# Row-half scores, a 0/1 mask product and a written instruction order in a sparse-attention plus mixer kernel

## The chip, the cores and the metric

The kernel runs on one core of one Trainium2 chip. The metric is the device time of one execution in microseconds (us). The kernel before takes 299.21 us, the median of three runs (299.06 to 299.65). A profile's span runs from the first to the last instruction and is some 2 us shorter than the time of the same execution.

## The reference, cut to what matters

```python
batch, n_heads, seq, head_dim = (4, 8, 768, 64)     # blocks of 32: 24 x 24 blocks
scores = q @ k.T / sqrt(D)
mask = |blk_i - blk_j| <= 1, first and last block row and column, 3 sampled blocks per row
attn = softmax(where(mask, scores, -1e9)) @ v
x = attn, heads side by side                        # (4, 768, 512)
u = x + (x.T @ U @ V).T                             # rank 32
out = u + relu(u @ w_ch1) @ w_ch2                   # 512 -> 2048 -> 512
```

Heads are handled in pairs: 4 pairs to a batch, 16 in all, numbered from 0.

## The kernel before: the parts that matter

The mask costs no instruction of its own in the steady state. Each head's transposed q and k fill 64 of the 128 rows that the array sums over. The other 64 rows hold a one-hot of the query block and a bias of -240 for masked block pairs, so one matmul gives score plus bias, and the exponential of a masked score is zero.

```python
def scores(i, h, g):                    # head h of pair i, 128 keys of row block g
    qT, kT = augs[i]                    # 64 data rows and 64 mask rows
    psc = pscp.tile([P, 2, 512], FP32, tag="psc", name="psc")   # 2 banks, double-buffered
    for c in range(2):
        nc.tensor.matmul(psc[:, c, 0:HS],
            kT[:, h, g * P : (g + 1) * P], qT[:, h, c * HS : (c + 1) * HS],
            start=True, stop=True)
    nc.scalar.activation(out=est[:, g]..., in_=psc[:, :, 0:HS], func=AF.Exp, scale=0.125)

def av(self, h, g): ...                 # value product: 6 matmuls of 65 columns a row block
def w1(jj, c): ...                      # hidden layer: 4 matmuls of 384 columns, then relu
def w2(sc, part): ...                   # output layer: 4 matmuls of 512 columns
# [cut]: PSUM pools: scores 2 x 2 banks, value product 1, everything else 3.
# [cut]: w1 and w2 steps are dealt evenly between the score slots of the next batch.
```

TensorE keeps the written order. On the other engines a scheduler chooses it, and the PSUM buffers come from pools.

The softmax here doesn't subtract the row's maximum and nothing guards it: scores larger than these inputs give would overflow.

## Time and profile before

| | before |
|---|---|
| time, median | 299.21 us |
| span | 296.7 us |
| TensorE, ScalarE, VectorE busy | 98%, 61%, 48% |
| exponentials, 768 columns | 192, one each 0.702 us where they follow each other |
| granted TensorE clock | 1.000 |

From the profile's page of the kernel before, the lines of busy time by engine and of the chain of waits (share of the span, by engine):

```profile
span 296.7 us, 6622 instructions
...
PE 291.4 (98%) x2775; PEld 182.3 (61%) x2775; DVE 142.0 (48%) x299; ACT 179.8 (61%) x261; POOL 50.2 (17%) x70
...
PE 87%; ACT 12%; issue 0%; DVE 0%
```

A busy TensorE is not yet a bound TensorE, so the chain is read next. It is followed backwards from the last instruction to whatever released each step. In order of time, for the kernel before (start, duration, engine, tile, line, count):

```profile
7.13 8.43 ACT est L392 x12
...
37.00 4.21 ACT est L392 x6
...
57.57 0.36 PE pv L426 x12
57.93 0.65 PE pm L509 x4
58.58 0.33 PE psc L386 x2
...
83.00 0.86 PE pm L531 x4
```

Until 42 us ScalarE is the chain: six exponentials take 4.21 us. From 48 us on only TensorE is on it, and these lines give its rates: 0.65/4 = 0.162 us for 384 columns, 0.86/4 = 0.215 us for 512, 0.36/12 = 0.030 us for a value-product matmul. The mean durations below are longer (325 ns for a score matmul) because matmuls overlap. Costs of TensorE must be taken from starts, not from durations.

Groups of the page: line, operation, shapes and count, then busy time and mean ns of one, then the idle time before them and its releaser.

```profile
L392 ACT ACTIVATE est<-psc 128x768 f16<-128x768 f32 x192 | 149.6, 812 | 51.6 <-PE psc L386 50.7
...
L386 PE MATMUL psc<-qres,kres 128*128 128x384 f16 x384 | 93.5, 325 | 1.0 <-ACT est L392 0.7
```

### The profile page before, as it was taken

What the parts mean: (1) busy time and instruction counts of PE and PEld (TensorE: products, weight loads), DVE (VectorE), ACT (ScalarE), POOL (GpSimd) and SP (SyncE); (2) the same over time, 40 slices, a digit from 0 to 9 for tenths busy, and PEclk for the clock granted to TensorE, in tenths of its full rate; (3) what the DMA queues carried; (4) which work ended last, traced back from release to release, by engine and by line L of the source; (5) the groups of instructions that cost most, each with busy time, mean ns of one, the idle gap of its engine ahead of it and who ended that gap; (6) DMA issues with size and microseconds to landing.
All of it is one profiled execution on the core that took longest, in us unless ns stands there. A gap on an engine that the chain in (4) does not pass through costs nothing.

```text
span 296.7 us, 6622 instructions
## 1 busy us (share of the span) xinstructions
PE 291.4 (98%) x2775; PEld 182.3 (61%) x2775; DVE 142.0 (48%) x299; ACT 179.8 (61%) x261; POOL 50.2 (17%) x70
## 2 busy tenths in 40 slices
PE   8999999999999999999999999999999999999995
PEld 3677776666666555666665556666665655565444
DVE  7766776346452525454452624346462535443112
ACT  5999997587766655767775555777875530332000
POOL 4773184014031212030201203030000000000000
PEclk9999999999999999999999999999999999999999
DMA  6899949096959494744719385662510121000111
GB/s 192 288 315 235 295 154 144 8 254 94 170 187 231 136 225 139 163 139 72 224 29 240 121 178 198 141 188 43 92 29 35 39 62 73 36 0 2 71 71 71
DMA packets 58661, 39.94 MB, mean 135 GB/s; under 512 B 40152, under 2 KB 55144, under 8 KB 58632
## 3 DMA queue, kind: packets, MB, share of 16 engines
q1 hardware_dynamic: 55764, 35.19, 43.9%
q0 software_dynamic: 2688, 4.19, 8.3%
q8 instruction: 21, 0.34, 0.5%
q10 hardware_dynamic: 180, 0.15, 0.1%
q14 instruction: 8, 0.07, 0.1%
HBM read 27.72 MB, written 6.29 MB: 115 GB/s over the span
## 4 chain that ended last, share of the span: by engine, by line
PE 87%; ACT 12%; issue 0%; DVE 0%
PE pm L509 28%; PE pm L531 27%; PE psc L386 16%; ACT est L392 12%; PE pv L426 9%; PE pm L448 1%; PE psc L218 1%; PE pm L481 1%; PE pm L550 1%; PE pm L527 0%; PE pm L497 0%; PE pm L364 0%; PE pm L201 0%; PE psc L201 0%; DVE of L555 0%
## 5 line engine op out<-in xcount | busy, mean ns | idle before, releaser
L392 ACT ACTIVATE est<-psc 128x768 f16<-128x768 f32 x192 | 149.6, 812 | 51.6 <-PE psc L386 50.7
L509 PE MATMUL pm<-uT,w1t 128*128 128x384 f16 x512 | 94.6, 326 | 0.0
L386 PE MATMUL psc<-qres,kres 128*128 128x384 f16 x384 | 93.5, 325 | 1.0 <-ACT est L392 0.7
L531 PE MATMUL pm<-w2t,tT 128*128 128x512 f16 x368 | 90.7, 379 | 0.0
L509 PEld LDWEIGHTS <-w1t 128*128 128x128 f16 x512 | 47.1, 98 | 27.0 <-issue 0.2
L426 PEld LDWEIGHTS <-est 128*128 128x128 f16 x1152 | 51.9, 97 | 16.5
L519 DVE TENSOR_SCALAR tT<-pm 128x384 f16<-128x384 f32 x64 | 35.6, 556 | 51.3 <-PE pm L509 48.6
L426 PE MATMUL pv<-vt,est 128*128 128x65 f16 x1152 | 55.7, 193 | 0.0
L517 ACT ACTIVATE tT<-pm 128x384 f16<-128x384 f32 x64 | 31.4, 490 | 38.2 <-PE pm L509 25.5
L386 PEld LDWEIGHTS <-kres 128*128 128x128 f16 x384 | 36.0, 97 | 27.0 <-issue 1.9
L531 PEld LDWEIGHTS <-tT 128*128 128x128 f16 x368 | 33.3, 98 | 30.1
L144 POOL CAST qst<-qld 128x768 f16<-128x768 f32 x10 | 8.3, 827 | 120.5 <-DMA qld<-in_q_dram 120.5
L539 DVE TENSOR_TENSOR of<-xf,pm 128x512 f32<-128x512 f32 x23 | 15.7, 684 | 25.9 <-PE pm L531 25.9
L435 DVE RECIPROCAL rcp<-pv 128x6 f32<-128x6 f32 x32 | 6.1, 192 | 38.1 <-PE pv L426 38.1
L440 DVE TENSOR_TENSOR xh<-pv,rcp 128x384 f16<-128x384 f32 x32 | 17.8, 557 | 1.0
L486 DVE TENSOR_TENSOR u<-xh,pm 128x384 f16<-128x384 f16 x24 | 13.2, 551 | 9.8 <-PE pm L481 9.3
L440 DVE TENSOR_TENSOR xf<-pv,rcp 128x384 f32<-128x384 f32 x32 | 17.5, 547 | 0.0
L154 POOL CAST vt<-vld 128x768 f16<-128x768 f32 x16 | 13.3, 828 | 14.7 <-DMA vld<-in_v_dram 14.2
L487 DVE TENSOR_TENSOR xf<-xf,pm 128x384 f32<-128x384 f32 x24 | 13.1, 547 | 0.0
L452 DVE CAST a<-pm 128x128 f16<-128x128 f32 x16 | 4.7, 291 | 15.9 <-PE pm L448 15.8
L144 POOL CAST kst<-kld 128x768 f16<-128x768 f32 x10 | 8.3, 827 | 5.1 <-DMA kld<-in_k_dram 5.1
L448 PE MATMUL pm<-xh,Ut 128*128 128x128 f16 x96 | 8.0, 219 | 0.0
(75 smaller groups left out, 111.2 us busy)
## 6 DMA issues: line engine op xcount, KB each, us to landing
vld<-in_v_dram SPq DMA_DIRECT2D x16, 384.0 KB, 5.3
out_dram<-of SPq DMA_DIRECT2D x23, 256.0 KB, 2.0
qld<-in_q_dram SPq DMA_DIRECT2D x15, 384.0 KB, 4.6
kld<-in_k_dram SPq DMA_DIRECT2D x15, 384.0 KB, 5.0
w1t<-in_moe_w_ch_dram POOLq DMA_DIRECT2D x4, 512.0 KB, 10.6
w2t<-in_moe_w_ch_dram POOLq DMA_DIRECT2D x4, 512.0 KB, 6.3
qld<-in_q_dram SPq DMA_DIRECT2D x2, 192.0 KB, 3.3
kld<-in_k_dram SPq DMA_DIRECT2D x2, 192.0 KB, 3.3
```

What stands on the lines that cost most here:

```text
L144: last = nc.gpsimd.tensor_copy(out=dst, in_=ld)
L154: nc.gpsimd.tensor_copy(out=vts[b % 2][:, 2 * hp : 2 * hp + 2, :, 0:D], in_=ld)
L386: nc.tensor.matmul(psc[:, c, 0:HS], kT[:, h, g * P : (g + 1) * P], qT[:, h, c * HS : (c + 1) * HS], start=True, stop=True,)
L392: nc.scalar.activation(out=est[:, g].rearrange("k (c n) -> k c n", c=2), in_=psc[:, :, 0:HS], func=AF.Exp, scale=0.125,)
L426: nc.tensor.matmul(pav[:, sc, :], est[:, g, sc * P : (sc + 1) * P], vts[self.b % 2][:, head, g, 0 : D + 1], start=(g == 0 and sc == 0), st ...
L440: self.last = nc.vector.tensor_tensor(out=dst, in0=pav[:, :, 0:D], in1=rcp[:, :, None].broadcast_to([P, T, D]), op=ALU.mult,)
L486: nc.vector.tensor_add(out=self.u16[:, ts, :], in0=self.xh[:, ts, :], in1=pu)
L509: nc.tensor.matmul(pt, w1t[:, cc, jj * P : (jj + 1) * P], bt.uT[cc][:, c * HS : (c + 1) * HS], start=(cc == 0), stop=(cc == NCC - 1),)
L517: nc.scalar.activation(out=dst, in_=pt, func=AF.Relu)
L519: nc.vector.tensor_scalar_max(out=dst, in0=pt, scalar1=0.0)
L531: nc.tensor.matmul(hold[sc], bt.tT[jj][:, sc * P : (sc + 1) * P], w2t[:, jj, :], start=(b > 0 and jj == 0), stop=(jj == NJJ - 1),)
L539: nc.vector.tensor_add(out=of, in0=bt.xf[:, sc, :], in1=hold[sc])
```

## The change

The intent is to take work off the bounding TensorE. From pair 4 on, a head's scores use only their 64 data rows, and the two heads of a pair stand in opposite halves of the array, to be multiplied at the same time. The mask can then no longer ride in the other rows. It is made once, by matmuls from zero-padded mask rows, as a 0/1 tile, and VectorE multiplies each exponential by it. One ScalarE instruction covers 1,536 columns. With the mask columns gone, the transposes of q and k by DMA are half as large. A "quad" below is two row blocks of both heads: eight matmuls, six of the eight PSUM banks, two exponentials, two mask products.

From pair 1's scores on, the order of all instructions on TensorE, ScalarE, VectorE and SyncE comes from a written string: a capital letter issues TensorE work, its digit names the PSUM bank, and a small letter issues the work that reads the result.

```diff
-    pscp, psvp, psmp: pools of 2 x 2, 1 and 3 banks
+    PS = psum.tile([P, 8, 512], FP32, name="ps")       # banks are named by hand
+    def psm(shape, dtype):
+        ring["psm"] += 1
+        return bank((7, 2, 5)[ring["psm"] % 3], shape, dtype)
...
+    def cast(i, dst, ld):
+        if i < NPE: return nc.gpsimd.tensor_copy(out=dst, in_=ld)
+        for h in range(2):                              # four pieces instead of one
+            for ts in (slice(0, T // 2), slice(T // 2, T)):
+                last = nc.gpsimd.tensor_copy(out=dst[:, h, ts], in_=ld[:, h, ts])
...
+    PLAN = """ ... Q b V7 e e U6 v p U3 a U4 a U7 p a U6 a Q a U7 e e U6 b V7 b
+    p U6 v p Q a W6 e e U7 p M3 b U4 m W a p D7 Q d W e e V7 p U3 v W a p Q f V7 e e ... """
...
+    def half_quad(i, j, hs):                            # "Q" calls it with hs = (0, 1)
+        for h in hs:
+            units[h] = PS[:, 3 * h : 3 * h + 3, :]...   # head 0: banks 0-2, head 1: 3-5
+        for u, lo, hi in ((0, 0, 512), (0, 512, S), (1, 0, 256), (1, 256, S)):
+            g = 2 * j + u
+            for h in hs:
+                nc.tensor.matmul(units[h][:, u * S + lo : u * S + hi],
+                    kT[drows[h], g * P : (g + 1) * P], qT[drows[h], lo:hi],
+                    start=True, stop=True, skip_group_check=True)
+        for h in hs:
+            def exps(h=h):                              # "e"
+                nc.scalar.activation(out=both[h], in_=units[h]..., func=AF.Exp, scale=0.125)
+                then("p", lambda: nc.vector.tensor_mul(  # "p"
+                    out=both[h], in0=both[h], in1=mask[:, 2 * j : 2 * j + 2, :]))
+            then("e", exps)
...
-                    elif i == 4: load_w2((0, 4))
-                    elif i == 5: load_w2((8, 12))
+                    elif i == 3: load_w2((0, 4))
+                    elif i == 4: load_w2((8, 12))
```

(Cut: the same value, mixer and layer steps as functions of a bank; K, the twelve mask products; R, transposes by TensorE; the interpreter of the string.)

In the string U is a hidden-layer product (four matmuls of 384 columns), W four matmuls of the output layer, V a head's value product, M and D the mixer, and a, b, v, d, f, m their readers.

## The prediction

> **What bounds the kernel now.** The chain of waits splits the 296.7 us span in two. Until 42 us ScalarE paces: its 768-column exponentials follow each other every 0.702 us. From 48 to 293 us the chain never leaves TensorE, which runs without a gap: 0.162 us per 384-column matmul, 0.86 us per four of 512, 0.030 us per value-product matmul (12 in 0.36 us). The granted clock is 1.0. VectorE is busy 48%, ScalarE 61%.
>
> **What the change removes and adds.**
> - Scores of pairs 4 to 15: the two heads become 64-row matmuls in opposite halves of the array. The Trainium skill ("TensorEngine Tiling (Array Packing)", Key Properties) says that tiles run in parallel and that a change of tiling mode drains the engine; no run shows the pairing yet. Today the same products cost 8 x 0.162 = 1.30 us; paired, 0.65 us plus two drains. In the trace the lone 24-row matmul among full ones costs 0.26 us for 384 columns, so about 0.1 us of switching; I take 0.75 us. Over 34 paired quads that takes about 19 us of TensorE away (the first four half-quads gain nothing).
> - Mask: 12 products of 384 columns, 2 us of TensorE, inside the stage that ScalarE bounds; 12 more evictions of 0.56 us on VectorE there.
> - Exponentials over 1,536 columns. From the trace (490 ns at 384, 812 at 768) one costs about 1.46 us, 1.35 back to back: a pair ends about 3.0 us after its scores.
> - 72 mask multiplications on VectorE. The skill ("VectorE: DVE Perf Modes", tier table) gives a 16-bit tensor_tensor 1.22 us for 2,048 columns; estimate 0.95 us, 68 us in all. VectorE rises to about 68%.
> - Half the transposes by DMA; W2 loads earlier; casts in quarters: no time by themselves.
>
> **Critical path.** TensorE work alone: first stage to about 46.5 us, then 163 us of quads with their fill, 60.6 us after the last quad, 3.5 us end: 274 us. But the quads take six of eight PSUM banks, and the written order gives banks 3 to 5 to other products early: in about 20 of 33 quads one of them stands only 1.5 to 1.9 us of TensorE work behind the quad, while those banks are freed by the second head's exponential, 3.0 us behind it (banks 0 to 2, free at 1.7 us, are not asked for before 3.0). The order looks as if made for the exponentials in the other sequence. Summed, that is 21 to 25 us of TensorE waiting: nearly all of the gain. Sum: 295 to 300 us of span, 297 to 302 us of time. Since such an order was presumably tried before it was kept, I pull it down a little.
>
> **Predicted: 297 us, 8 in 10 between 284 and 306. Faster by over 2%: 0.33; within 2%: 0.54; slower by over 2%: 0.13.**
>
> **What would show it.** Score matmuls of the two heads starting together, a quad in 0.65 to 0.85 us. TensorE waiting on the exponential before hidden-layer products into the shared banks: 15 to 28 us in total, holes of about 1.2 us. Exponentials near 1.46 us, multiplications near 0.95 us. First quad near 46 us, about 60 us after the last. ScalarE about 60% busy.
>
> **What would make it wrong.** Shorter holes, because TensorE work before the wait lasts longer than its rate or ScalarE finishes earlier: 275 to 285 us. Pairs that do not overlap: up to 20 us more. Multiplication at one result a cycle (1.7 us): VectorE would bound the quads, 310 us. GpSimd casts blocking VectorE.

## More of the kernel before

From its timeline:

```profile
6.61 0.48 PE L386 MATMUL psc<-qres,kres 128*128 128x384 f16 x2
6.93 0.50 PE L281 MATMUL pm<-id,stqld 128*128 128x128 f16 x6
7.07 0.56 DVE L233 CAST kres<-pm 24x384 f16<-24x384 f32 x1
7.13 1.51 ACT L392 ACTIVATE est<-psc 128x768 f16<-128x768 f32 x2 [1.02 <-PE psc L386]
```

The transposes of the second head (L281) follow the first scores at once, and the second exponential follows the first.

## The result, and the profile after

| | before | after |
|---|---|---|
| time, median (range) | 299.13 us (298.53 to 299.65) | 313.15 us (312.24 to 314.08) |
| ratio, 95% interval | | 1.0471 (1.0438 to 1.0503) |
| span | 296.7 us | 312.1 us |
| TensorE busy / on the chain | 98% / 87% | 91% / 66% |

A ratio is the mean time of one kernel's fast runs over that of the other's in the same rounds, so it is not quite the ratio of the medians. The runs of before are those of its own measurement and of the rounds beside the change. The change costs 4.7%.

The same lines of the page, after:

```profile
span 312.1 us, 6725 instructions
...
PE 283.1 (91%) x2769; PEld 165.1 (53%) x2769; DVE 190.1 (61%) x341; ACT 186.6 (60%) x224; POOL 70.2 (23%) x157
...
PE 66%; ACT 24%; issue 4%; DVE 2%; DMA 2%; ACTq 0%; DVEq 0%
```

TensorE now does less, and it is also less busy in a longer span: it waits. What it waited for between 52 and 262 us, the stage of the quads (engine, line, releaser: us in total, times, longest):

```profile
PE ps L575 <- ACT est L712: 13.3, 15, 1.1
PE ps L507 <- ACT est L712: 4.2, 4, 1.0
PE ps L575 <- DMA uT<-u: 3.2, 1, 3.2
PE ps L413 <- ACT est L712: 0.2, 1, 0.2
```

L712 is the exponential of 1,536 columns, L575 the hidden layer, L507 the mixer. The chain around one quad (L703) shows such a wait:

```profile
68.84 0.80 PE ps L703 x8
69.64 2.79 ACT est L712 x2
72.43 0.04 issue
72.47 0.49 PE ps L507 x6
72.96 0.65 PE ps L575 x4
```

The chain leaves TensorE for both exponentials, 2.79 us, and returns with the mixer product "M3", which needs bank 3. It can start only when the second head's exponential has read that bank. In the trace, 20 products of this kind start some 2.9 us after the recorded end of their quad, whatever came between, and TensorE stands 20.8 us before them (start to start, less the rates above; the list has 17.7 us, because it counts from the recorded ends of the matmuls).

The groups of the new work:

```profile
L712 ACT ACTIVATE est<-ps 128x1536 f16<-128x1536 f32 x72 | 100.6, 1448 | 38.2 <-PE ps L703 38.1
...
L718 DVE TENSOR_TENSOR est<-est,mask 128x1536 f16<-128x1536 f16 x72 | 69.4, 971 | 17.6 <-ACT est L712 17.6
...
L703 PE MATMUL ps<-qpl,kpl 64*128 64x512 f16 (+1 forms) x288 | 31.3, 325 | 0.8 <-ACT est L687 0.8
```

Two more losses were in no estimate. The first is the start; these lines answer to those of before:

```profile
6.65 0.48 PE L397 MATMUL ps<-qres,kres 128*128 128x384 f16 x2
7.11 1.60 DVE L246 CAST kres<-ps 24x384 f16<-24x384 f32 x3
7.17 0.81 ACT L403 ACTIVATE est<-ps 128x768 f16<-128x768 f32 x1 [1.02 <-PE ps L397]
...
8.76 0.49 PE L294 MATMUL ps<-id,stqld 128*128 128x128 f16 x6 [1.63 <-DVE kres L246]
...
9.62 0.81 ACT L403 ACTIVATE est<-ps 128x768 f16<-128x768 f32 x1 [1.64 <-PE ps L397]
```

The second head's transposes (now L294) wait 1.63 us for VectorE to read the mask rows. The pool had given them a bank that was free; the hand-made ring 7, 2, 5 comes round to the bank that holds the mask rows. The second exponential starts at 9.62 us.

The second loss is a transpose by DMA. Timeline of the change from 122 to 133 us, cut to SyncE's issues and what waits:

```profile
122.44 1.26 SPq L350 DMA_TRANSPOSE qpl<-stqld  x1
...
123.30 0.56 DVE L548 TENSOR_TENSOR u<-xh,ps 128x384 f16<-128x384 f16 x1 [0.48 <-PE ps L541]
...
123.80 1.63 SPq L350 DMA_TRANSPOSE kpl<-stkld  x1
...
126.61 0.76 SPq L163 DMA_DIRECT2D vld<-in_v_dram  x1
...
127.47 1.22 SPq L553 DMA_TRANSPOSE uT<-u  x1
...
132.60 0.65 PE L575 MATMUL ps<-uT,w1t 128*128 128x384 f16 x3 [3.21 <-DMA uT<-u]
```

The input u of the transpose is ready at 123.9 us (L548), but SyncE issues the transpose at 127.5, after two transposes and three loads that were written ahead of it, and TensorE's product waits until 132.6 us. From 1.1 us after this wait of 3.4 us (start to start; the list above has 3.2) the hidden-layer matmuls start 0.32 us apart instead of 0.162 for about 3.4 us, which adds 1.7 us. The slice holding it is the page's only one with a granted clock of seven tenths. The Trainium skill ("TensorE: Matmul & The Clock Gate", Part 1) has the clock halved after an idle window of about 3.4 us; the runs agree only in part. The matmuls are slow behind waits of 3.4 us here, 4.3 us in e1 below and 3.3 us in e3, and not behind one of 3.2 us in e2. But e2 has a slow stretch of the same length from 9.7 us on (its page shows seven tenths in the second slice), behind a wait of only 1.6 us. What sets such a stretch off is not settled by these runs.

### The profile page after: what moved, and what is told of

It reads as the page before. It is cut to its first block, busy times and chain, and to the rows that moved or that the text cites. A ratio compares the mean times of both kernels' runs of the same rounds, so it can differ in the third digit from the quotient of the medians.

```text
span 312.1 us, 6725 instructions
## 1 busy us (share of the span) xinstructions
PE 283.1 (91%) x2769; PEld 165.1 (53%) x2769; DVE 190.1 (61%) x341; ACT 186.6 (60%) x224; POOL 70.2 (23%) x157
## 4 chain that ended last, share of the span: by engine, by line
PE 66%; ACT 24%; issue 4%; DVE 2%; DMA 2%; ACTq 0%; DVEq 0%
PE ps L575 26%; PE ps L602 20%; ACT est L712 14%; PE ps L703 9%; ACT est L687 7%; PE ps L413 5%; DMA uT<-u 2%; ACT est L403 2%; PE ps L507 2%; PE ps L541 1%; PE ps L622 1%; DVE kres L246 1%; DMA small<-small_const 1%; PE ps L397 0%; ACT L255 0%
## 5 line engine op out<-in xcount | busy, mean ns | idle before, releaser
L712 ACT ACTIVATE est<-ps 128x1536 f16<-128x1536 f32 x72 | 100.6, 1448 | 38.2 <-PE ps L703 38.1
L575 PE MATMUL ps<-uT,w1t 128*128 128x384 f16 x512 | 95.6, 330 | 16.6 <-ACT est L712 13.3
L585 ACT ACTIVATE tT<-ps 128x384 f16<-128x384 f32 x99 | 48.5, 491 | 69.1 <-PE ps L575 68.4
L602 PE MATMUL ps<-w2t,tT 128*128 128x512 f16 x368 | 88.9, 379 | 0.0
L718 DVE TENSOR_TENSOR est<-est,mask 128x1536 f16<-128x1536 f16 x72 | 69.4, 971 | 17.6 <-ACT est L712 17.6
L575 PEld LDWEIGHTS <-w1t 128*128 128x128 f16 x512 | 48.9, 99 | 52.6 <-issue 23.0
L413 PE MATMUL ps<-vt,est 128*128 128x65 f16 x1152 | 43.9, 193 | 0.2 <-ACT est L712 0.2
L703 PE MATMUL ps<-qpl,kpl 64*128 64x512 f16 (+1 forms) x288 | 31.3, 325 | 0.8 <-ACT est L687 0.8
L687 ACT ACTIVATE est<-ps 128x768 f16<-128x768 f32 x36 | 26.6, 809 | 0.5 <-PE ps L678 0.5
L703 PEld LDWEIGHTS <-kpl 64*128 64x128 f16 x288 | 11.8, 94 | 14.8 <-issue 8.5
L481 DVE TENSOR_TENSOR xh<-ps,rcp 128x384 f16<-128x384 f32 x32 | 17.8, 557 | 1.1
L144 POOL CAST stkld<-kld 128x192 f16<-128x192 f32 x40 | 18.0, 490 | 1.8 <-DMA kld<-in_k_dram 1.7
L548 DVE TENSOR_TENSOR u<-xh,ps 128x384 f16<-128x384 f16 x24 | 13.2, 550 | 5.8 <-PE ps L541 5.7
```

The source lines that it names most:

```text
L144: last = nc.gpsimd.tensor_copy(out=dst[:, h, ts], in_=ld[:, h, ts])
L413: nc.tensor.matmul(pav[:, sc, :], est[:, n, sc * P : (sc + 1) * P], vts[b % 2][:, 2 * hp + h, g, 0 : D + 1], start=(g == 0 and sc == 0), s ...
L481: self.last = nc.vector.tensor_tensor(out=dst, in0=pav[:, :, 0:D], in1=rcp[:, :, None].broadcast_to([P, T, D]), op=ALU.mult,)
L575: nc.tensor.matmul(pt, w1t[:, cc, jj * P : (jj + 1) * P], bts[b].uT[cc][:, c * HS : (c + 1) * HS], start=(cc == 0), stop=(cc == NCC - 1),)
L585: nc.scalar.activation(out=dst, in_=pt, func=AF.Relu)
L602: nc.tensor.matmul(po, tts[b, c, jj][:, s * P : (s + 1) * P], w2t[:, jj, :], start=(b > 0 and jj == 0), stop=(jj == NJJ - 1), skip_group_c ...
```

## The experiments

Each kernel is the changed one with the edit shown, run beside the kernel before on the same chip; e8 to e12 start from e7. The change itself did not run beside them: its 313.15 us is compared across rounds, in which the median of the kernel before was 299.02 to 299.33 us.

Each execution also has a mean granted clock. A slow stretch of 3.4 us, as above, lowers it by about 0.0055 (an estimate: half of 3.4 us in 310 us) and costs about 1.7 us. Of the change's four executions, two had a clock of 1.000 (312.24 and 312.56 us), two of 0.993 and 0.995 (314.08 and 313.75 us).

### e1: the second head's exponential first

```diff
-        for h in hs:
+        for h in reversed(hs):
             def exps(h=h):
```

> The changed kernel with one thing altered: the exponential of the second head (banks 3 to 5) is issued ahead of that of the first (banks 0 to 2); no other instruction moves. Theory A (the order was made for that sequence; TensorE stands in 20 holes of 1.0 to 1.3 us until 2.94 us after each quad, some 24 us in all, because banks 3 to 5 are freed last): the holes of over 0.8 us behind a quad vanish, the rest shrinks below 4 us, and the time falls by 20 to 26 us, to 287 to 293 us. Rival B (VectorE's 72 mask products and evictions hold TensorE back, the exponentials only happen to be the last wait): the time falls by less than 6 us.

Measured: 293.38 us (292.42 to 295.39), ratio 0.9817 (0.9774 to 0.9861) to before: under 1 beyond the noise, and unclear by the record's margin of 2%; span 292.2 us, 19.9 less than the change. The chain over the same quad as above, now L703 at 67.17 us:

```profile
67.17 0.76 PE ps L703 x8
67.93 0.32 PE ps L595
...
69.12 0.65 PE ps L575 x4
69.77 0.33 PE ps L507 x6
```

No exponential is on it any more. The 20 holes are gone; the one wait of TensorE left in this stage is for the transpose:

```profile
PE ps L575 <- DMA uT<-u: 4.1, 1, 4.1
```

The fall of 19.8 us in the median lies just under the expected 20 to 26, and that wait is 0.9 us longer in this execution than in the change's. Swapping the two exponentials of each quad turns a loss of 4.7% into a gain of 1.8%, so the order of banks in the string fits this sequence and not the other. (The two mask products of a quad follow their exponentials and swap with them, which the expectation overlooked; e2 shows that they do not matter.) Why the string was written so is not known.

### e2: no mask product (a wrong result, on purpose)

```diff
-                then("p", lambda: nc.vector.tensor_mul(out=both[h], in0=both[h], in1=mask[...]))
+                then("p", lambda: None)
```

> The changed kernel without the 72 mask multiplications (a wrong result, on purpose), which takes 69 us off VectorE and nothing off the other engines. Theory A (bank order): the holes behind the quads end at the same 2.94 us, the time falls by less than 3 us. Rival B (VectorE bounds the quads): the time falls by 15 us or more.

Measured: 314.22 us (313.71 to 315.67), span 311.7 us. TensorE's waits in the quads, with VectorE at 41%:

```profile
PE ps L575 <- ACT est L712: 13.4, 15, 1.1
PE ps L507 <- ACT est L712: 4.4, 4, 1.1
PE ps L575 <- DMA uT<-u: 3.1, 1, 3.1
...
```

Taking 69 us of work off VectorE takes nothing off the time: rival B falls.

### e3: the bank ring advanced by one

```diff
     def last_turn(n):
+        if n == 0: ring["psm"] += 1
         pt = psm([P, S], FP16)
```

> The changed kernel with the fixed ring of PSUM banks advanced by one before the first pair's second-head transposes, so that they don't fall on the bank that holds the mask rows. Theory: the 1.63 us wait of TensorE for VectorE at 7 to 8.7 us, which only the fixed ring made, goes; the second exponential starts near 8.0 us instead of 9.6, and the time falls by 1.2 to 2.5 us. Rival: the first stage is bound elsewhere (VectorE's mask evictions), and the time falls by less than 0.6 us.

Measured: 314.6 us (312.66 to 316.36), which overlaps the change's own range and is no gain. Its two longest executions, over 316 us, had a clock of 0.989; the one at 1.000 took 312.66 us, where the change's two took 312.24 and 312.56 us. In the trace the wait is gone, and the transposes follow the scores again:

```profile
7.16 0.49 PE L399 MATMUL ps<-qres,kres 128*128 128x384 f16 x2
7.48 0.50 PE L296 MATMUL ps<-id,stqld 128*128 128x128 f16 x6
```

The first paired quad comes 0.9 us earlier (51.58 against 52.46 us) although the first exponential of that execution came 0.5 us later. The mechanism is shown, its worth in time is not; see e11.

### e4: the transpose ahead of the loads

```diff
+        if i == 9: held.append(i)            # begin(9): leave its loads
+        else: loads(i)
...                                           # and in "d", behind the transpose of uT:
+                    while held: loads(held.pop())
```

> The changed kernel with the loads that begin with pair 9 queued on SyncE behind, not ahead of, the transpose of the last pair of the second batch. Theory: the wait of 3.4 us of TensorE at 129 us for that transpose goes, and with it the half-speed clock of the next 3.4 us (1.6 us): the time falls by 4 to 5.5 us, to 308 to 309 us. Rival (the transpose is late because its input is): it falls by less than 1 us.

Measured: 311.38 us (310.34 to 311.43), ratio 1.0402 (1.0382 to 1.0422); span 308.4 us, 3.7 less than the change.

```profile
123.41 0.55 DVE L548 TENSOR_TENSOR u<-xh,ps 128x384 f16<-128x384 f16 x1 [0.48 <-PE ps L541]
...
123.99 1.44 SPq L553 DMA_TRANSPOSE uT<-u  x1
...
130.69 2.60 PE L577 MATMUL ps<-uT,w1t 128*128 128x384 f16 x15 [1.03 <-ACT est L714]
```

In this execution the wait for the DMA and the slow matmuls behind it are gone. The expectation was too high because a hole of 1.2 us that the longer wait had covered stands there now: 3.4 + 1.7 - 1.2 = 3.9 us, close to the 3.7 us between the spans. The medians differ by only 1.8 us, and the clock tells why: this execution had 0.999, but e4's other three had 0.994, as one slow stretch somewhere would make it. At like clocks e4 gains 1.9 to 2.2 us (310.34 against 312.24 and 312.56 us) and 2.3 to 2.7 us (311.37 to 311.43 against 313.75 and 314.08 us). That is the 3.4 - 1.2 = 2.2 us of the wait; the slow stretch is not reliably taken away.

### e7 and e13: the three together

```diff
+ the edits of e1, e3 and e4
```

> The changed kernel with the three alterations together: second head's exponential first, the bank ring skipped by one, the transpose ahead of the loads. Theory (the three losses are what separates the change from its promise, and they add): the span falls from 292.2 us with the swap alone by the hole of 4.3 us and its clock of 1.4 us, and by up to 1 us at the start, to 285.5 to 287.5 us; the time is 286 to 289 us, 3.5 to 4.5% under the kernel before. Rival (another limit takes over, for instance VectorE at some 67% busy): it stays above 291 us.

> The kernel with all three alterations once more, as the neighbour of the next two on one chip: 286.9 us again, within 0.3%.

Measured: 286.85 us (286.44 to 287.27), ratio 0.959 (0.9577 to 0.9603); the second time 287.28 us (286.93 to 289.69), ratio 0.9618 (0.9587 to 0.965). The times are as expected; the span of the first, 284.5 us, lies 1.0 us under the expected range, and in the second two of six executions, at clocks of 0.994 and 0.988, took over 289 us. Both kernels are beaten: 4% under before, 8% under the change. The page of the first:

```profile
span 284.5 us, 6716 instructions
...
PE 277.5 (98%) x2769; PEld 164.5 (58%) x2769; DVE 188.8 (66%) x341; ACT 184.8 (65%) x224; POOL 69.8 (25%) x157
...
PE 85%; ACT 11%; issue 1%; DMA 1%; DVE 1%; POOL 0%; ACTq 0%
```

TensorE is back at 98%, in a span 12 us shorter than before's.

### e8: casts whole again

```diff
-        if i < NPE:
+        if i < NPAIR:
             return nc.gpsimd.tensor_copy(out=dst, in_=ld)
```

> The kernel with all three alterations, and the casts whole again instead of in quarters. Theory (casts and two-operand VectorE instructions hold each other up, so that quarters keep the waits of VectorE short): mask products that overlap a cast get longer, but as TensorE has slack to VectorE here, the time changes by less than 0.5%. Rival: a whole cast delays an eviction enough to stop TensorE, and the time rises by 1% or more.

Measured: 287.67 us (287.23 to 288.37) against 286.85 for e7 beside it, 0.3% more, with intervals that touch. The mean mask product grew from 974 to 1,013 ns, and one eviction came late enough to hold TensorE (0.46 us in the list of waits):

```profile
77.23 3.08 PE L579 MATMUL ps<-uT,w1t 128*128 128x384 f16 x18 [0.46 <-DVE of L614]
```

The Trainium skill ("SBUF — State Buffer", Who interferes with whom) says that a VectorE instruction with two SBUF inputs contends with a GpSimd instruction that reads SBUF. The numbers agree: in the trace of e8 the 16 mask products that overlap a cast take 1.22 us in the mean, the other 56 take 0.95 us. The casts in pieces are at most a small help here, not a cause of the loss.

### e9: W2 loads back in their old place

```diff
-                elif i == 3: load_w2((0, 4))
-                elif i == 4: load_w2((8, 12))
+                elif i == 4: load_w2((0, 4))
+                elif i == 5: load_w2((8, 12))
```

> The kernel with all three alterations, and the W2 loads back with pairs 4 and 5 instead of 3 and 4. The first output product starts 15 to 25 us after the first quad. Theory: with the later loads it waits for its weights by DMA, and the time rises by 1 to 6 us. Rival: the weights land in time anyway, no change over 0.5 us.

Measured: 287.39 us (287.03 to 288.34), 0.5 us over e7, with intervals that overlap. The profile has the wait, once:

```profile
75.39 1.02 PE L606 MATMUL ps<-w2t,tT 128*128 128x512 f16 x4 [0.65 <-DMA w2t<-in_moe_w_ch_dram]
```

The mechanism is as expected, and it is worth less than a microsecond.

### e10: the heads of a quad one after the other

```diff
-        for u, lo, hi in (...):
-            for h in hs:
+        for h in reversed(hs):
+            for u, lo, hi in (...):
```

> The kernel with all three alterations, and in each quad the four matmuls of one head first and then the four of the other, instead of alternating; the same instructions. Theory (the halves of the array run together only when matmuls of the two halves stand side by side): a quad takes 1.3 to 1.4 us of TensorE instead of 0.76, and the time rises by 34 times 0.55 to 0.65 us, 17 to 21 us, so that the change would lose all its gain. Rival (TensorE pulls the other half's matmuls forward by itself): the time rises by less than 3 us.

Measured: 287.77 us (287.58 to 288.22), 0.9 us over e7 where 17 to 21 us were expected: my theory falls. Starts of the eight matmuls of one quad in the trace, in us from the first, worked out from the start times:

```
alternating (e7):      0.000  0.004 | 0.227  0.230 | 0.336  0.339 | 0.445  0.449
one head, then other:  0.000  0.013 | 0.227  0.240 | 0.336  0.349 | 0.445  0.458
```

In the second row the matmul that started after 0.013 us is the fifth in the program. (The trace has no program counter; the built program holds the four matmuls of one head and then those of the other, as written.) So TensorE starts work for the free half of the array ahead of earlier matmuls that wait for the busy half. Pairing does not need alternation.

### e11 and e12: the ring, and the mask product, where the rest is dense

e11 is e7 without the ring's edit; e12 is e7 with the edit of e2 (a wrong result).

> All three alterations but the bank ring left as the change has it. Alone, over the unsteady changed kernel, the ring's worth did not show in the times (314.6 us against 313.15) though the first quad came 0.9 us earlier. Theory: the 1.6 us wait at the start is worth 0.8 to 1.8 us where the rest is dense: 287.7 to 288.7 us, against 286.9. Rival: worth nothing, within 0.4 us of its neighbour.

> All three alterations without the 72 mask products (a wrong result, on purpose). Theory (TensorE bounds it, VectorE has slack in every quad): the time falls by less than 1 us. Rival (with the holes gone VectorE is next): it falls by 4 us or more.

Measured: e11 288.34 us (287.56 to 288.88), ratio 0.9632 (0.9612 to 0.9652), against 287.28 for e13 beside it. This is 1.1 us in the expected direction, but the intervals overlap. Part of the spread is the clock: the executions at 1.000 took 287.56 to 288.34 us in e11 (three) and 286.93 to 287.28 us in e13 (four), so the ring is worth some 0.7 us there, a little under the expected 0.8 to 1.8. e12: 286.89 us (286.34 to 287.87), 0.4 us under e13 with intervals that overlap. The mask products cost nothing that shows: VectorE has room.

## Why the prediction was right or wrong

It was wrong: 297 us with a range to 306 was predicted, 313.15 measured. The chances put 0.13 on slower by over 2%. The sum of the critical path, term by term, with what the trace of the change shows (TensorE's starts; waits are taken beyond its rates):

| term | predicted, us | measured, us |
|---|---|---|
| start to the first paired quad | 46.5 | 52.5 |
| 33 quads, with the switch of tiling | 24.8 (0.75 each) | 28.2 (0.76 and 0.10) |
| other work between the quads | 138.3 | 139.7 |
| waits for banks 3 to 5 | 21 to 25 | 20.8 |
| wait for the transpose by DMA | 0 | 3.4 |
| slow matmuls behind it, other small gaps | 0 | 2.8 |
| from the last quad to TensorE's end | 60.6 | 61.2 |
| end | 3.5 | 3.6 |
| span | 295 to 300 | 312.1 |

e7 tests the sum without its waits. Its list of TensorE's waits between the quads is empty, and still the span is 284.5 us where the prediction's sum without waits was 274: the first paired quad comes at 51.2 us instead of 46.5, the quads and the work between them take 169.0 us instead of 163, the rest 64.3 us instead of 64.1. So the waits for banks were estimated rightly, on a base that was set over 10 us too low.

- **The mechanism that decides, right.** TensorE's saving is eaten by waits, mostly of 0.9 to 1.3 us, for banks that the second head's exponential frees some 2.9 us after the quad. About 20 holes and 21 to 25 us were predicted; 20 holes and 20.8 us were measured. e1 shows the cause, and e2 excludes the mask products.
- **The step that failed first: "first stage to about 46.5 us", which was 52.5.** In the kernel before the 48th exponential ends at 41.3 us, so 46.5 left about 5.2 us from there to the first paired quad. In the trace of the change the 48th ends at 44.5 us, where the first half-quad starts: late by the wait on the bank ring (1.6 us), by the mask evictions and copies of VectorE, on which the chain stands from 17.7 to 19.2 us, and by exponentials that follow each other every 0.73 us after that instead of 0.71. How much each of the last two is worth was not tested. From there to the first paired quad there are 8.0 us of nearly gapless TensorE work (7.2 us at the rates above, the rest switches of tiling and short waits), and the sum left much of it out.
- **"Half the transposes by DMA; W2 loads earlier; casts in quarters: no time by themselves": failed in one point.** The new written order on SyncE puts loads ahead of the transpose that TensorE needs: 3.4 us of waiting, 1.7 us of slow matmuls. e4 takes the wait away, of which 2.2 us reach the time. The Trainium skill ("DMA: Bandwidth & Descriptors", Queues, rings and completion order) says that descriptors are consumed in ring order on each DMA engine. The trace agrees as far as the issue goes: the transpose goes out 3.6 us after its input is ready, behind two transposes and three loads. The other two points held (e8, e9).
- **The switch of tiling mis-sized.** I took 0.1 us for it and the trace shows 0.10 us before and 0.11 us behind, 0.21 us a quad. The quads cost 3.4 us more than estimated.
- **The pull.** I lowered a sum of 297 to 302 us because such an order was presumably tried before it was kept. That was a guess about people against an argument from the trace, and it had the wrong sign.
- **Sizes that held.** Exponential 1.46 us, measured 1.448; mask product 0.95, measured 0.971; ScalarE 60% busy. "A quad in 0.65 to 0.85 us" and the heads starting together hold: 0.76 us, 3 to 4 ns apart.

Apart from the waits for banks, the terms of the table came out 17.7 us longer in sum, and that is more than the half-width of the range, 11 us. The range should have been skewed upwards: every unlisted wait in a hand-written order lengthens a chain in which nothing was slack.

## What to carry to other kernels

When a change moves the bound from work to order, list for each shared buffer who frees it and when, and compare that with how much work stands between; here that count alone gave the main loss to within a few us. A hand-written order can hang on one sequence of releases, here 19.8 us on that of two exponentials: test it by swapping them. And replacing pools and a scheduler with fixed rings and queues brings new waits in places the change was not about, such as the start and the DMA issue queue; leave room for them in an estimate.

## What the Trainium skill lacked or had wrong

- "TensorE: Matmul & The Clock Gate", Part 3, What overlaps and what doesn't: it has matmuls in strict first-in-first-out order with no reordering. e10 shows that across halves of the array they are not: the fifth matmul of the program started 13 ns after the first, 0.21 us before the second, and the whole kernel lost 0.9 us where the estimate for serial halves was 17 to 21.
- "TensorEngine Tiling (Array Packing)", Key Properties: it says that a change of tiling mode drains TensorE and gives no figure. Measured: 0.10 us before the first 64-row matmul and 0.11 us behind the last, beyond the rate, at each of 34 quads. Where it says that tiles work in parallel the trace agrees: eight matmuls in 0.76 us, four of one head alone in 0.74 us.
- "DMA: Bandwidth & Descriptors" gives the order within a ring; what it costs a short transpose behind loads, the runs show: 5.1 us from issue to use behind three loads of 384 KB, where the median to landing of all eleven transposes of this tile in the change is 3.6 us, and of before's nine 2.8.
